# VectorE's order at the start of an attention and FFN kernel, and what TensorE multiplies only to be busy

## The chip, the cores and the metric

The kernel runs on one core of a Trainium2 chip. A core has engines with a queue of instructions each: TensorE (PE, matrix products; PEld is its loading of the stationary operand), VectorE (DVE), ScalarE (ACT), GpSimd (POOL) and SyncE (SP), which here issues nearly all transfers. Engines wait for each other through semaphores. The metric is the device time of one launch in microseconds; lower is better.

## The reference

For each of 8 batches and 8 heads, 576 positions of q, k and v (64 wide) go through a feature map with 128 random features, linear attention, and then a two-layer FFN over all 4,608 tokens.

```python
def phi(x):
    proj = np.einsum('bhsd,md->bhsm', x, omega)
    sq = np.sum(x * x, axis=-1, keepdims=True) / 2.0
    h = proj - sq
    h = h - np.max(h, axis=-1, keepdims=True)
    return np.exp(h) / np.sqrt(m)
q_p, k_p = (phi(q_s), phi(k_s))
kv = np.einsum('bhsm,bhsd->bhmd', k_p, v)
z = np.sum(k_p, axis=2)
num = np.einsum('bhsm,bhmd->bhsd', q_p, kv)
den = np.einsum('bhsm,bhm->bhs', q_p, z)[..., None] + 1e-06
x = num / den                       # as (4608, 512)
h = x @ w_in                        # 512 x 2048
g = h * np.tanh(softplus(h))
out = g @ w_out                     # 2048 x 512
```

## The kernel before

Tokens go in 36 query tiles of 128 (`q0` to `q35`) and 18 FFN blocks of 256. Keys go by batch and pair of heads (`k0_0` is batch 0, pair 0). Most products take operands that are split into two float16 parts; the first work runs on float32 instead, because the splits need scales that are not known yet: all keys of batches 0 and 1 and the queries of tiles 0 to 4, their products with the values, and FFN block 0.

**A key or query tile** (`features`, L376): the load is popped from those made at the start; TensorE multiplies it with `om_f` into banks of PSUM (`pk`, `pq`, L416); VectorE takes the maximum of each row (L426); ScalarE takes the exponentials with the maximum as bias (L431). In the float32 tiles two to five (`1 < nth < 6`: k0_2, k0_3, q0, q1), `spin(1, ident, e...)` (L443) then multiplies a part of the result by the identity into a bank that nobody reads. `spin` (L98) issues such unread products; there are also ten at the start, eight behind the second key tile (L422), both from the constant `idle`, and two behind the x of tile 1 (L709). The function ends with `anchors[nth] = (last.ins, sub.ins)`: the tile's last exponential (ScalarE) and its last maximum (VectorE).

**Keys** then go into a product with the values (`pkv`, L490), which ScalarE copies out (L496). **Queries** (`q_first`, L658): TensorE transposes the exponentials (`pt`, L665), ScalarE copies them (L666), TensorE multiplies them with the key-value sums (`pn`, L676), VectorE divides (L680 to L692) into `x`; for tiles 0 and 1, TensorE transposes x (`px`, L703) and ScalarE copies it to `xT` (L704). That is what the first FFN product (`ph`, L770) needs, together with w_in.

**w_in** comes in eight blocks of 1 MB, w0 to w7 (`w_task`, L200): ScalarE brings one part of each word into place (L211), VectorE shifts the other (L213), joins the two by an or (L217) and takes the block's maximum (L221). From all eight maxima comes the scale by which the blocks are split for the float16 blocks that follow. The values of batch 0 have a like step: `v_task` (L309) takes four maxima (L319) and from them a scale.

**Order.** The program is written as a list of generators that are stepped slot by slot (`step`, L1190); a yield says in how many slots a generator goes on. FIRST, WIS and WOS (L1135 to L1137) say in which slot a tile or weight block starts. Within a slot the generators go in the order in which they were put on the list: first `v_task(0)`, then the weight blocks, then the key and query tiles, which are put on it later. A planner then orders each engine's queue: among instructions that it counts as ready, the earlier in the program goes first; the engine executes that order as it stands. `with behind(nth, first)` (L194) adds an order without a semaphore: what is issued inside comes, on its own engine, behind the instructions `anchors[nth][first:]` of the same engine. The tables AV, AN, AM, AO, AP (L1141 to L1145) say for each block behind which anchor its steps come: AV for the values' maxima, AN for the shift and the or, AM for the blocks' maxima, AP for ScalarE's step. `anchors[30 + t]` is the x of tile t on VectorE, `anchors[100 + t]` its copy on ScalarE.

**Transfers.** PREL (L1149) lists the first loads: keys, values, q0, q1, then the eight blocks of w_in; q2, q3 and the values of batch 1 follow on the same queue.

**PSUM.** The pool `ps_a` has four banks and serves pk, pq, pkv, pt, pn and px; `ps_h` (two) serves ph and one bank of each of the first key tiles; `ps_o` (two) serves the FFN's outputs and the spins. The exponentials lie in two buffers (tag `ae`).

Of the kernel before, what the change touches and what calls it, by code (L numbers as in the profile page):

```python
# [30 lines left out]
def tile_kernel(  # L31
# [10 lines left out]
    nc = tc.nc  # L42
    P = 128
# [27 lines left out]
    def cast(eng, out, in_, scale=1.0):  # L71

        if eng is act:
            act.activation(out, in_, AF.Copy, scale=scale)  # L74
        elif isinstance(scale, float) and scale == 1.0:
            eng.tensor_copy(out, in_)  # L76
        else:
            eng.tensor_scalar_mul(out, in_, scale)
# [16 lines left out]
    idle = const.tile([P, 512], F16, name="idle")  # L95
    dve.memset(idle, 1.0)

    def spin(n, left, right):  # L98
        pi = ps_o.tile([P, 512], F32, tag="o", name=f"spin{nc.next_id()}")
        for _ in range(n):  # L100
            nc.tensor.matmul(out=pi[:, 0:right.shape[1]], lhsT=left, rhs=right, start=True, stop=True)
# [3 lines left out]
    ident = const.tile([P, P], F32, name="ident")  # L105
# [87 lines left out]
    @contextmanager  # L193
    def behind(nth, first=0):  # L194
        with ExitStack() as st:
            for ins in anchors.get(nth, ())[first:]:
                st.enter_context(tc.issue_after(ins))
            yield

    def w_task(i, name):  # L200

        n = 0 if name == "wi" else 1
        raw = loaded.pop(f"w{n}_{i}", None) or fetch_w(n, i, w_dma)
        yield W_LOAD
        word = raw.bitcast(I32).rearrange("p (n two) -> p n two", two=2)
        low, high = word[:, :, 0], word[:, :, 1]
        dst = flat32(slots[w_at(n, i)])
        di = dst.bitcast(I32)
        with behind(AP[i] if n == 0 else None):
            m = high.bitcast(F32)  # L210
            act.activation(m, m, AF.Prelu, scale=2.0 ** -112, alpha=-(2.0 ** 32))  # L211
        with behind((AN, AO)[n][i]):
            dve.tensor_single_scalar(out=di, in_=low, scalar=29, op=ALU.logical_shift_right)  # L213
        yield W_GAP
        did("w", n, i)
        with behind((AN, AO)[n][i]):
            dve.scalar_tensor_tensor(  # L217
                out=di, in0=high, scalar=3, in1=di, op0=ALU.logical_shift_left, op1=ALU.bitwise_or
            )
        with behind(AM[i] if n == 0 else None):  # L220
            dve.tensor_reduce(  # L221
                out=wmax[n][:, i:i + 1], in_=dst, axis=AX.X, op=ALU.max, apply_absolute_value=True
            )
# [70 lines left out]
    for i in range(2):  # L294
        t = const.tile([P, 2, 10, D1], F16, name=f"vb{i}")
# [13 lines left out]
    def v_task(b):  # L309
        vt = []  # L310
        for hp in range(HP):
            vt.append(loaded.pop(f"v{b}_{hp}", None) or fetch_v(b, hp))
        if b == 0:
            vstate[0] = (vt, None, None)
        yield 3 if b else 6
        mx = sb.tile([P, HP], F32, tag="vmx", name=f"vmx{b}", bufs=2)
        for hp in range(HP):
            with behind(AV if b == 0 else None, 1):
                dve.tensor_reduce(  # L319
                    out=mx[:, hp:hp + 1], in_=vt[hp][:, :, 0:D], axis=AX.XY, op=ALU.max,  # L320
                    apply_absolute_value=True,
                )
            yield 0 if hp % 2 == 0 or b == 0 else 1
        am = sb.tile([P, 1], F32, tag="vam", name=f"vam{b}")
        if b < 2:
            with tc.high_priority(PRIO):
                dve.tensor_reduce(out=am, in_=mx, axis=AX.X, op=ALU.max)
                p, s = pow2(am, f"v{b}", TOP)
        else:
            dve.tensor_reduce(out=am, in_=mx, axis=AX.X, op=ALU.max)  # L330
            yield 1
            p, s = yield from pow2_pe(am, f"v{b}", TOP)
        vstate[b] = (vt, p, s)
# [5 lines left out]
    anchors = {}  # L339
# [36 lines left out]
    def features(load, tiles, name, nth, whole):  # L376

        f = loaded.pop(name, None) or (  # L380
            fetch_pair if whole else fetch_tails if name[0] == "k" else fetch
        )(load, name)
        yield gap("load", name)
        if not whole:
            terms = yield from in_parts(f, name, nth)
        n = sum(len(g) for g in tiles)
        by_act = whole
        e = sb.tile([P, n, M], F32, tag="ae", name=f"e{name}", bufs=2)
        mx = sb.tile([P, n], F32, tag="mx", name=f"mx{name}")
        pps, lo = [], 0  # L390
        for g in tiles:
            own, tag = (ps_h, "h") if nth < HP and len(pps) == 2 else (ps_a, "a")
            pp = own.tile([P, 4, M], F32, tag=tag, name=f"p{name}_{lo}")
            pps.append((pp, lo, lo + len(g)))
            lo += len(g)
            if whole:
                continue
            for i, parts in enumerate(g):
                for rows, o in parts:
                    for j, (left, right) in enumerate(terms):  # L400
                        nc.tensor.matmul(  # L401
                            out=pp[rows, i, :], lhsT=left[:, o:o + rows.stop - rows.start],
                            rhs=right, start=j == 0, stop=j == len(terms) - 1,
                        )
        if whole:

            w = f.shape[1]
            order = [(g, i) for i in range(4) for g in (0, -1)] + [(1, 0)] * (len(tiles) - 2)
            mm = None
            for g, i in order:  # L410
                for rows, o in tiles[g][i]:
                    a = slice(o // w * D, (o // w + 1) * D)
                    with ExitStack() as st:
                        if mm is not None:
                            st.enter_context(tc.issue_after(mm.ins))
                        mm = nc.tensor.matmul(  # L416
                            out=pps[g][0][rows, i, :], lhsT=f[a, o % w:o % w + rows.stop - rows.start],
                            rhs=om_f[a], start=True, stop=True,
                        )
            if nth == 1:  # L420
                with tc.issue_after(mm.ins):
                    spin(8, idle[:, 0:P], idle)  # L422
        yield 1
        for pp, lo, hi in pps:
            m = hi - lo
            sub = dve.tensor_reduce(  # L426
                out=mx[:, lo:hi], in_=pp[:, :m, :], axis=AX.X, op=ALU.max, negate=by_act
            )
            if by_act:
                for i in range(m):  # L430
                    last = act.activation(  # L431
                        e[:, lo + i, :], pp[:, i, :], AF.Exp, bias=mx[:, lo + i:lo + i + 1]
                    )
            else:
                sub = dve.tensor_tensor(  # L435
                    out=e[:, lo:hi, :], in0=pp[:, :m, :],
                    in1=mx[:, lo:hi].unsqueeze(2).broadcast_to([P, m, M]), op=ALU.subtract,
                )
        yield gap("exp", name)
        if not by_act:  # L440
            last = act.activation(e, e, AF.Exp, bias=lnt)  # L441
        elif 1 < nth < 6:
            spin(1, ident, e[:, 0:2, :].rearrange("p n m -> p (n m)"))  # L443
        anchors[nth] = (last.ins, sub.ins)
        return e

# [95 lines left out]
    def q_task(nth, t):  # L542
# [5 lines left out]
        e = yield from features(qT[t], tiles, f"q{t}", nth, t < QF)  # L548
        if t < QF:
# [9 lines left out]
            out=qp.rearrange("p a h s -> p (a h) s"), in_=qn.rearrange("p a h m -> p (a h m)")  # L559
# [18 lines left out]
        for g, pn in enumerate(pns):  # L578
# [10 lines left out]
                out=x[:, hs, :], in0=pn[:, :, 0:D], in1=rd[:, hs].broadcast_to([P, 4, D]),  # L589
                op=ALU.mult,  # L590
            )
        anchors[30 + t] = (xt.ins,)
        yield from x_parts(nth, t, x)

    x_more = {}
# [62 lines left out]
    def q_first(nth, t, e, off):  # L658

        qp = sb.tile([P, H, P], F32, tag="ap", name=f"qp{t}", bufs=2)  # L660
        for g in range(2):
            hs = slice(4 * g, 4 * g + 4)
            pt = ps_a.tile([P, 4, P], F32, tag="a", name=f"pt{t}_{g}")
            for i in range(4):
                nc.tensor.transpose(out=pt[:, i, :], in_=e[:, 4 * g + i, :], identity=ident)  # L665
            cast(act, qp[:, hs, :], pt)  # L666
        yield 1
        x = sb.tile([P, H, D], F32, tag="x", name=f"x{t}", bufs=2)
        rd = sb.tile([P, H, 1], F32, tag="rd", name=f"rd{t}")
        for g in range(2):  # L670
# [20 lines left out]
            for b, lo, hi in spans(t * P, P):  # L691
# [1 line left out]
                    out=x[lo:hi, hs, :], in0=pn[lo:hi, :, 0:D], scalar=vstate[b][2][lo:hi],  # L693
                    in1=rd[lo:hi, hs].broadcast_to([hi - lo, 4, D]), op0=ALU.mult, op1=ALU.mult,
                )
        anchors[30 + t] = (xt.ins,)
        if t * P >= CH:
            yield from x_parts(nth, t, x)
            return
# [433 lines left out]
    w_dma = nc.sync  # L1133

    FIRST = (0, 1, 2, 3, 4, 4, 9, 9, 19, 21, 24, 27, 32, 36, 43, 58, 59, 68)  # L1135
    WIS = (3, 4, 5, 6, 7, 8, 9, 10)
    WOS = (28, 27, 26, 25, 24, 23, 22, 21)  # L1137
    WI0, FF0, V0, V1 = 0, 17, 0, 16
    W_LOAD, W_GAP, PRIO = 1, 1, 400

    AO = (None,) * 8  # L1141
    AV = 3
    AN = (None,) * 5 + (31,) * 3
    AM = (None,) * 3 + (31,) * 5
    AP = (None,) * 7 + (101,)  # L1145

    W_LO = ('dddddddd', 'dddddddd')
# [91 lines left out]
    for what in PREL.split():  # L1239
        i = int(what[1:] or 0)  # L1240
# [105 lines left out]
```

## Time and profile before

| what | value |
| --- | --- |
| median of three runs | 939.56 us (939.08 to 940.1) |
| the profiled execution | 939.57 us |
| its span, from the first to the last instruction | 937.8 us |
| mean granted clock of TensorE | 0.993 |

An execution on the chip is recorded instruction by instruction. The page of the profile gives the busy time of each engine, the chain of work that ended last, and groups of instructions. Lines of a timeline read: start, length, engine, line, operation, what is written and from what, shapes, count, and in brackets how long the engine had been idle before it and what ended that. Instructions of one engine can overlap by a fraction in the record, so a group's time is better read from one start to the next. Rows of windows give busy times in a stretch of the span, the TensorE clock that was granted (1.00 is full), the share of the transfer engines and GB/s.

### The profile page before, as it was taken

Reading aid. Unit: us, or ns where it says so; the run is one execution under the profiler, and the core shown is the slowest. Engines: PE = TensorE matmul, PEld = TensorE weight load, DVE = VectorE, ACT = ScalarE, POOL = GpSimd, SP = SyncE. Lnnn points to the kernel's source line nnn. Section 1 sums busy time; section 2 is a strip of 40 time slices with the busy share of each in tenths; the row PEclk is TensorE's granted clock in tenths of the full one; section 3 lists DMA queues with packets and bytes.
Section 4 is the critical chain, followed back from the end, with each engine's and each line's share of the span. In section 5 each row is a group of like instructions: output and inputs, shape, how many; then the busy total and the mean of one; then the engine's idle time right before and its main releaser. Section 6 shows DMA issues by size and latency. Waiting matters only on the chain. (4 is left out here: it accounts for less than half of the span.)

```text
span 937.8 us, 21111 instructions
## 1 busy us (share of the span) xinstructions
PE 920.5 (98%) x8795; PEld 689.4 (74%) x8795; DVE 707.1 (75%) x1234; ACT 658.9 (70%) x873; POOL 213.6 (23%) x134
## 2 busy tenths in 40 slices
PE   9799989999999999999999999999999999999998
PEld 6688765677777777777777777777777777679997
DVE  5799898685678688787688857878688756658774
ACT  6568966678777878778677776788786866345442
POOL 0000023242342224321333134231241232200000
PEclk9799999999999999999999999999999999999999
DMA  9766325443442256323543265523533156973521
GB/s 308 264 227 215 108 58 93 99 83 75 95 107 85 80 115 128 90 81 76 107 114 97 69 120 107 126 60 93 112 73 91 35 114 141 210 218 92 162 66 45
DMA packets 153055, 108.69 MB, mean 116 GB/s; under 512 B 112832, under 2 KB 125248, under 8 KB 152960
## 3 DMA queue, kind: packets, MB, share of 16 engines
q1 hardware_dynamic: 152640, 106.75, 44.6%
q8 instruction: 69, 1.13, 0.5%
q10 hardware_dynamic: 320, 0.59, 0.2%
q14 instruction: 26, 0.21, 0.1%
HBM read 63.14 MB, written 17.83 MB: 86 GB/s over the span
## 5 line engine op out<-in xcount | busy, mean ns | idle before, releaser
L770 PE MATMUL ph<-xT,w 128*128 128x256 f16 (+1 forms) x2816 | 342.2, 278 | 0.0
L1097 PE MATMUL po<-wo,g 128*128 128x512 f16 x1344 | 308.5, 379 | 0.0
L770 PEld LDWEIGHTS <-w 128*128 128x128 f16 x2688 | 260.7, 98 | 46.1 <-issue 0.6
L1097 PEld LDWEIGHTS <-g 128*128 128x128 f16 x1344 | 127.2, 98 | 132.7
L83 POOL TENSOR_TENSOR sq<-fq,sq 64x1024 f16<-64x1024 f32 x31 | 70.5, 2275 | 253.6 <-ACT sq L74 177.8
L955 ACT ACTIVATE h<-ph,us 128x512 f32<-128x512 f32 (+3 forms) x152 | 83.2, 573 | 49.7 <-PE ph L770 48.5
L85 DVE SCALAR_TENSOR_TENSOR g<-h,us,g 128x1024 f16<-128x1024 f32 (+3 forms) x76 | 99.9, 1325 | 15.2 <-ACT g L74 14.9
L83 POOL TENSOR_TENSOR sk<-fk,sk 64x1152 f16<-64x1152 f32 x24 | 59.3, 2469 | 91.6 <-ACT sk L74 79.3
L83 POOL TENSOR_TENSOR xs<-x,xs 128x512 f16<-128x512 f32 (+1 forms) x35 | 40.7, 1164 | 153.0 <-DVE xs L76 102.0
L955 ACT ACT_TABLE_LOAD x56 | 71.8, 1283 | 1.0
L441 ACT ACT_TABLE_LOAD x53 | 68.0, 1283 | 4.2 <-DVE ek L435 3.3
L426 DVE TENSOR_REDUCE mxq<-pq 128x4 f32<-128x512 f32 x72 | 46.7, 682 | 24.8 <-PE pq L401 23.9
L83 DVE TENSOR_TENSOR qn<-eq,qn 128x1024 f16<-128x1024 f32 x31 | 39.2, 1263 | 29.9 <-ACT qn L74 29.9
L906 PEld LDWEIGHTS <-w 128*128 128x128 f16 x1008 | 59.0, 98 | 3.3 <-issue 0.7
L441 ACT ACTIVATE ek<-ek,lnt 128x1152 f32<-128x1152 f32 x24 | 30.1, 1256 | 42.3 <-DVE ek L435 42.2
L74 ACT ACTIVATE g<-h,us 128x1024 f16<-128x1024 f32 (+3 forms) x64 | 58.2, 932 | 0.8
L426 DVE TENSOR_REDUCE mxk<-pk 128x4 f32<-128x512 f32 (+1 forms) x96 | 49.5, 546 | 7.3 <-PE pk L416 3.5
L83 DVE TENSOR_TENSOR kp<-ek,kp 128x1152 f16<-128x1152 f32 x24 | 32.8, 1366 | 27.0 <-ACT kp L74 26.2
L1044 PEld LDWEIGHTS <-gb 128*128 128x128 f16 x504 | 48.3, 98 | 5.2
L83 POOL TENSOR_TENSOR vb<-vf,vb 128x640 f16<-128x640 f32 x24 | 37.3, 1554 | 55.2 <-DVE vb L76 41.5
L955 ACT ACTIVATE h<-h,us 128x1024 f32<-128x1024 f32 (+2 forms) x16 | 14.7, 930 | 48.6 <-DVE h L915 48.6
L441 ACT ACTIVATE eq<-eq,lnt 128x1024 f32<-128x1024 f32 x31 | 35.6, 1149 | 18.8 <-DVE eq L435 18.5
(185 smaller groups left out, 1370.3 us busy)
## 6 DMA issues: line engine op xcount, KB each, us to landing
w<-ds SPq DMA_DIRECT2D x48, 256.0 KB, 3.6
vf<-in_vL_dram SPq DMA_DIRECT2D x32, 325.0 KB, 3.3
out_dram<-o SPq DMA_DIRECT2D x36, 256.0 KB, 2.3
fq<-in_qT_dram SPq DMA_DIRECT2D x31, 256.0 KB, 3.5
fk<-in_kT_dram SPq DMA_DIRECT2D x24, 256.0 KB, 3.6
raw<-in_w_out_dram SPq DMA_DIRECT2D x5, 1024.0 KB, 7.8
wo<-in_w_in_dram SPq DMA_DIRECT2D x4, 1024.0 KB, 10.6
raw<-in_w_in_dram SPq DMA_DIRECT2D x4, 1024.0 KB, 15.3
```

The lines of the kernel that those rows point to most:

```text
L74: act.activation(out, in_, AF.Copy, scale=scale)
L83: eng.tensor_tensor(out=out, in0=in_, in1=hi, op=ALU.subtract)
L85: eng.scalar_tensor_tensor(out=out, in0=in_, scalar=scale, in1=hi, op0=ALU.mult, op1=ALU.subtract)
L426: sub = dve.tensor_reduce(out=mx[:, lo:hi], in_=pp[:, :m, :], axis=AX.X, op=ALU.max, negate=by_act)
L441: last = act.activation(e, e, AF.Exp, bias=lnt)
L770: nc.tensor.matmul(out=ph[:, i, :], lhsT=wi(a, k, f) if c else wi0(k, f), rhs=xT[c][:, y, k, :] if c else xT0()[:, k, :], start=n == 0, st ...
L906: nc.tensor.matmul(out=ph[:, i, :], lhsT=left(gr, op_l, i, a, k), rhs=x_region(c, r)[:, y, k0 + k, :], start=n == 0, stop=n == len(mm) - 1,)
L955: act.activation(h[:, :, lo:hi], ph[:, :, lo:hi], AF.Mish, scale=us[:, 0:1])
L1044: nc.tensor.matmul(out=ps, lhsT=gT[c, n][:, i, a, f, :], rhs=rhs, start=f == 0 and (a, y) == (1, 0), stop=f == FG - 1 and (a, y) == (0, 0),)
L1097: nc.tensor.matmul(out=po[i], lhsT=gT[c, gr][:, a, f % FG, i * P:(i + 1) * P], rhs=wo(y, f), start=f == 0 and (a, y) == parts[0], stop=f = ...
```

## The change

Three things are rewritten at the start of the kernel.

VectorE's order: `AN` is split into `AS` (for the shift) and `AN` (for the or). w0's or and maximum and w1's shift now come behind the last maximum of tile 3 (k0_3); w1's or and maximum, w2's shift and maximum, and the values' maxima (AV) behind the last maximum of tile 5 (q1). Blocks 5 to 7 stay behind the x of tile 1 (31). All blocks of w_in start one or two slots later (WIS), the values' maxima one slot later.

`behind` for VectorE's steps now takes the anchor's second entry (`first=1`), so `anchors[30 + t]` gets a `None` in front.

The unread products: the four that read exponentials are removed; behind the transposes of query tiles 0 and 1 come four each from the constant `idle`, 512 wide.

```diff
-        with behind((AN, AO)[n][i]):
+        with behind((AS, AO)[n][i], 1):
             dve.tensor_single_scalar(out=di, in_=low, scalar=29, op=ALU.logical_shift_right)
         yield W_GAP
         did("w", n, i)
-        with behind((AN, AO)[n][i]):
+        with behind((AN, AO)[n][i], 1):
             dve.scalar_tensor_tensor(
...
-        with behind(AM[i] if n == 0 else None):
+        with behind(AM[i] if n == 0 else None, 1):
             dve.tensor_reduce(
...
-        yield 3 if b else 6
+        yield 3 if b else 7
...
-        elif 1 < nth < 6:
-            spin(1, ident, e[:, 0:2, :].rearrange("p n m -> p (n m)"))
         anchors[nth] = (last.ins, sub.ins)
...
-        anchors[30 + t] = (xt.ins,)
+        anchors[30 + t] = (None, xt.ins)
...
             for i in range(4):
-                nc.tensor.transpose(out=pt[:, i, :], in_=e[:, 4 * g + i, :], identity=ident)
+                tr = nc.tensor.transpose(out=pt[:, i, :], in_=e[:, 4 * g + i, :], identity=ident)
             cast(act, qp[:, hs, :], pt)
+        if t < 2:
+            with tc.issue_after(tr.ins):
+                spin(4, idle[:, 0:P], idle)
...
-    WIS = (3, 4, 5, 6, 7, 8, 9, 10)
+    WIS = (4, 6, 7, 8, 9, 10, 11, 12)
...
-    AV = 3
-    AN = (None,) * 5 + (31,) * 3
-    AM = (None,) * 3 + (31,) * 5
+    AV = 5
+    AS = (None, 3, 5) + (None,) * 2 + (31,) * 3
+    AN = (3, 5) + (None,) * 3 + (31,) * 3
+    AM = (3, 5, 5) + (31,) * 5
```

More of the change, by code (lines that the diff above doesn't have):

```diff
@@ L695, in q_first @@
                 )
-        anchors[30 + t] = (xt.ins,)
+        anchors[30 + t] = (None, xt.ins)
         if t * P >= CH:
```

## The prediction, made before the changed kernel was run

> **What bounds the kernel now.** The profiled execution took 939.57 us, 1.77 us more than its span, against a median of 939.56 us; a microsecond less of span is taken as one off the time. I read the page first, then TensorE's waits, windows around the longest wait, and the timelines of TensorE, VectorE and ScalarE there.
>
> ```profile
> span 937.8 us, 21111 instructions
> PE 920.5 (98%) x8795; PEld 689.4 (74%) x8795; DVE 707.1 (75%) x1234; ACT 658.9 (70%) x873; POOL 213.6 (23%) x134
> ...
> PE spin L101 <- ACT eq L431: 6.9, 1, 6.9
> ...
> 22.70:29.60 6.90, 0.00 (x1) 0.01 (x1) 6.63 (x14) 3.31 (x7) 0.62 (x1) 0.64 1.06 389
> 29.60:38.30 8.70, 8.70 (x36) 7.85 (x36) 6.96 (x8) 5.03 (x14) 0.00 (x0) 0.50 1.06 327
> 160.00:937.80 777.80, 772.56 (x7751) 577.02 (x7748) 571.15 (x995) 542.69 (x660) 197.41 (x109) 1.00 0.43 102
> ...
> 24.00:25.00 1.00, 0.00 (x0) 0.00 (x0) 1.00 (x3) 0.18 (x1) 0.00 (x0) 0.84 1.04 385
> 38.00:39.00 1.00, 1.00 (x6) 0.53 (x5) 0.00 (x0) 1.00 (x4) 0.00 (x0) 0.84 1.03 330
> ```
>
> (Window rows: stretch, length, busy time of PE, PEld, DVE, ACT, POOL, granted clock, DMA share, GB/s.) TensorE bounds the kernel: behind 160 us it is busy 772.56 of 777.80 us. So time is won only where it stands still early, and there is one such place: it waits 6.9 us for the exponentials of q0, and the granted clock falls. 0.84 in 24 to 25 is full speed until 24.7 and half after, 2.0 us behind the last matmul; 0.84 in 38 to 39 puts the return at 38.3, after 8.7 us of work at half speed, half of which (4.35 us) is loss. Stall and clock together cost 6.9 + 4.35 = 11.3 us.
>
> ```profile
> 15.73 0.65 PE L101 MATMUL spin<-ek,ident 128*128 128x256 f32 x2
> 16.31 1.53 PE L416 MATMUL pk<-om_f,fk 64*128 64x128 f32 x20
> 17.76 2.45 PE L490 MATMUL pkv<-vf,ek 128*128 128x65 f32 x20
> 20.05 0.65 PE L101 MATMUL spin<-ek,ident 128*128 128x256 f32 x2
> 20.63 2.06 PE L416 MATMUL pq<-om_f,fq 64*128 64x128 f32 x32
> 29.60 1.22 PE L101 MATMUL spin<-eq,ident 128*128 128x256 f32 x2 [6.92 <-ACT eq L431]
> 30.61 4.37 PE L490 MATMUL pkv<-vf,ek 128*128 128x65 f32 x20
> 34.77 1.06 PE L665 MATMUL pt<-ident,eq 128*128 128x128 f32 x4
> 35.69 1.22 PE L101 MATMUL spin<-eq,ident 128*128 128x256 f32 x2
> 36.71 2.85 PE L665 MATMUL pt<-ident,eq 128*128 128x128 f32 x12
> ...
> 17.55 0.69 DVE L426 TENSOR_REDUCE mxk<-pk 128x4 f32<-128x512 f32 x1 [0.38 <-PE pk L416]
> 18.16 1.21 DVE L217 SCALAR_TENSOR_TENSOR w<-wo,w 128x1024 int32<-128x1024 int32 x1
> 19.29 0.28 DVE L426 TENSOR_REDUCE mxk<-pk 128x1 f32<-128x128 f32 x1
> 19.50 1.21 DVE L221 TENSOR_REDUCE wmax<-w 128x1 f32<-128x1024 f32 x1
> 20.62 0.68 DVE L213 TENSOR_SCALAR w<-wo 128x1024 int32<-128x1024 int32 x1
> 21.22 0.68 DVE L426 TENSOR_REDUCE mxk<-pk 128x4 f32<-128x512 f32 x1
> 21.82 2.98 DVE L319 TENSOR_REDUCE vmx<-vf 128x1 f32<-128x640 f32 x4
> 24.72 1.21 DVE L217 SCALAR_TENSOR_TENSOR w<-wo,w 128x1024 int32<-128x1024 int32 x1
> 28.14 0.68 DVE L426 TENSOR_REDUCE mxq<-pq 128x4 f32<-128x512 f32 x1
> ...
> 28.92 2.17 ACT L431 ACTIVATE eq<-pq,mxq 128x128 f32<-128x128 f32 x8 [1.99 <-DVE s_v L127]
> 35.02 0.62 ACT L431 ACTIVATE eq<-pq,mxq 128x128 f32<-128x128 f32 x2 [2.88 <-PE pkv L490]
> ```
>
> The products of q0 and q1 are there at 22.69, but VectorE takes their first maximum at 28.14. Ahead of it stand the values' maxima (2.98 us) and shift, or and maximum of w_in's blocks. That is an order of the queue, not lack of data, and the change rewrites it.
>
> **The old spins go.** Four spins hang on exponentials. The first two take 0.58 us each from start to next start (15.73 to 16.31, 20.05 to 20.63); the two on eq take 1.0 us each at half clock, 0.5 at full. Without the first two, pk of k0_3 starts at 15.7 and the products of q0, q1 end at 22.69 - 1.16 = 21.5. Pool `ps_a` has four banks; counted through the code, the values' product of k0_3 needs a bank that q0's first four exponentials free. So removing the spin alone doesn't remove the wait (gain of that alone between 0 and 1.2 us).
>
> **The new order on VectorE.** w0's or and maximum and w1's shift now come behind k0_3's maxima, which then end near 15.7 + 1.2 (16.31 to 17.55) + 0.69 + 0.28 + 0.68 = 18.5 instead of 21.9. w0's pair, earlier in program order than q0's maxima, probably still goes first: 18.5 + 1.2 + 1.2 = 20.9. q0's first maximum is then at 20.9; its bounds are 20.5 (half of the products done, nothing ahead) and 21.5 (w1's shift too). The first four exponentials take half of 2.17: 21.6 to 22.7. The values' product of k0_3 runs from 22.7, 7.9 us earlier than 30.61, at full clock in 2.3 us (17.76 to 20.05), to 25.0. TensorE's stall shrinks from 6.9 to 1.2 us, below the 2.0 us after which the clock fell, so I take the clock as full.
>
> **The rest of the way to FFN block 0.** eq of q1 waits for that product (2.88 us in its row) and still will.
>
> ```profile
> 39.39 3.68 PE L676 MATMUL pn<-kvf,qp 128*128 128x65 f32 x32
> 45.18 0.48 PE L416 MATMUL pq<-om_f,fq 64*128 64x128 f32 x2
> 45.60 0.70 PE L770 MATMUL ph<-xT,w 128*128 128x256 f32 x2
> 46.23 2.05 PE L416 MATMUL pq<-om_f,fq 64*128 64x128 f32 x30
> ...
> 7.98 1.90 PE L101 MATMUL spin<-idle 128*128 128x512 f16 x8
> 9.96 0.17 DVE L146 MEMSET idle<- 1x128 f32 x1 [0.77 <-PE spin L101]
> ```
>
> From the end of the product (34.77) to the first ph (45.60) are 10.83 us. Half clock until 38.3 makes up 3.53 / 2 = 1.77 us of it; an old spin of 0.5 goes; eight new ones come, 1.90 us by the row of eight. They read only a constant and stand where TensorE waits for ScalarE to copy pt and finish q1's exponentials, so their cost lies between 0 and 1.9; I take 1.4. The memset of `idle` at 9.96 must now wait for them, 0.2 us of VectorE beside the x chain. The first ph: 25.0 + 10.83 - 1.77 - 0.5 + 1.4 = 35.0, which is **10.6 us earlier**.
>
> **What is moved behind.** The four values' maxima and w1's or and maximum, w2's shift, wait behind q1's last maximum, about 23.4 (20.9 + four of 0.6 from start to start); behind them on VectorE stand w2 to w4 and then q0's x. The value loads of batch 1 wait for those tiles, but SP reaches them only at 29.51. w1 is read by ph's third f, well behind 35. If its order is bad, one such instruction (1.2 us) stands ahead of x; between 0 and 1.2, taken as 0 because x is earlier in program order.
>
> **How much of 10.6 us reaches the end.** TensorE is the bound later, but VectorE is nearly as full in between.
>
> ```profile
> 17.50:44.10 26.60, 19.45 (x137) 17.19 (x138) 21.36 (x41) 16.64 (x39) 0.62 (x1) 0.74 0.93 319
> 44.10:160.00 115.90, 112.44 (x777) 83.80 (x775) 108.02 (x184) 89.56 (x145) 14.32 (x10) 1.00 0.47 139
> ```
>
> VectorE's work up to 44.1 fills 21.36 of 26.60 us: it can come only 5.2 us earlier. From there to 160 it idles 7.88 us more, which it may give up. So its shift lies between 5.2 and 13.1, TensorE's is 10.6. I let VectorE give up half: 5.2 + 3.9 = 9.1 us. Fillers for TensorE (FFN block 0's products, the other products of block 1) are at hand meanwhile, so VectorE's lag isn't all paid: 5.2 is the low end, 10.6 the high. **Forecast: 939.6 - 9.1 = 930.5 us, 929 to 934.4.**
>
> **Rivals.** *A load becomes the wait.* In TensorE's order the first products of q2 stand ahead of the first ph (45.18 before 45.60).
>
> ```profile
> L361 SPq DMA_DIRECT2D fq<-in_qT_dram x4: 589/596/2585, 25.0 to 28.9; - x4
> 29.51 8.95 SPq L306 DMA_DIRECT2D vf<-in_vL_dram  x4
> DMA to landing us min/median/max: 11.4/11.6/13.8
> ```
>
> These loads of q2 and q3 are issued behind all of w_in (first at 25.0, last at 28.9) and land at 25.0 + 13.8 = 38.8, the last at 28.9 + 11.4 = 40.3. Before, that was early enough; now TensorE could stand at q2 from 35.0 to 38.8, 3.8 us, over the 2.0 after which the clock fell. Against it: the queue orders are planned, and a planner that counts this load late puts ph first. The first ph would be near 40.3, a gain of 5.3 where the clock holds; at half for 8.7 us of work, as here, it costs 4.35 of them, gain 0.95. Between the two, **936.4 us**. [...] *Slower:* the same stall, but the clock stays at half as long as here, 24.7 to 38.3 = 13.6 us: 6.8 lost, 5.3 - 6.8 = -1.5, **941.1 us**. The load decides once the stall at q2 exceeds 2.0 us, and the sign turns once the clock stays at half for more than 2 x 5.3 = 10.6 us.
>
> [...]
>
> *The change doesn't bite*: the planner takes what is ready, w blocks slip ahead of q0 as before, and only the spins count: gain 0 to 1.2, **939.0 us**.
>
> **How the numbers follow.** Forecast 0.60; more than 10.6 us (idle later also filled, down to 926.5) 0.05; load without the long half clock 0.14; clock falls 0.08; doesn't bite 0.04; slower 0.09. 0.2% is 1.9 us, about what a measurement tells from no change. Faster: 0.60 + 0.05 + 0.08 and 0.09 of the load's 0.14, 0.82; same: its other 0.05 and the 0.04, 0.09; slower: 0.09. The range 926.5 to 937.0 takes in the forecast, its better tail, the fallen clock and half of the load; the rest is 0.20.
>
> **What would show it.** Right: mxq of q0 near 21, directly behind w0's or k0_3's work; no TensorE gap over 2 us from 15 to 45; granted clock 1.00 in every microsecond from 10 on; first ph near 35; the same landmarks at 160 us some 9 us earlier. Wrong: a wait of pq for fq near 35 to 39; a clock below 1 in 25 to 50; VectorE's last maximum of w_in less than 5 us earlier; or new waits of TensorE between 60 and 160 that add up to more than 5 us.

## The result, and the profile after

| | before | after |
| --- | --- | --- |
| median | 939.83 us (939.08 to 940.65, 6 runs) | 946.08 us (943.88 to 948.07, 6 runs) |
| the profiled execution | 939.57 us | 947.22 us |
| its span | 937.8 us | 945.4 us |
| its mean granted clock | 0.993 | 0.990 |

The ratio is 1.0064 [1.0053, 1.0074]: the change makes the kernel about 6 us slower. The six runs of after spread over 4.2 us, and the fastest (943.88) is the one with the highest mean clock (0.993); the others have 0.988 to 0.990. A kernel's queues are planned once, the falls of its clock differ from execution to execution (mean clock 0.988 to 0.993 in these six). At a mean clock of 0.993, the commonest in before (939.8 and 940.0 us, the medians of 13 such runs in each of the two sets below), after's one run still takes 4 us more, so the clock is only a part of the difference.

First TensorE's waits in the profile of after (who waited for whom: us in total, times, longest):

```profile
PE pn L570 <- DMA qp<-qn: 5.3, 3, 4.3
PE pn L570 <- DVE ek L435: 2.9, 1, 2.9
PE pk L416 <- ACT ek L431: 2.5, 1, 2.5
PE pkv L488 <- ACT eq L431: 1.6, 1, 1.6
```

The wait of 6.9 us at the start is gone but for 1.6. Three longer ones stand in its place, all of them later: for exponentials of a key tile, for a transposed operand, and for a key tile from which VectorE takes the maxima off (`ek`, L435). TensorE's timeline of after shows where:

```profile
1.47 4.45 PE L101 MATMUL spin<-idle 128*128 128x512 f16 x10 [1.47 <-DVE idle L96]
20.45 2.06 PE L416 MATMUL pq<-om_f,fq 64*128 64x128 f32 x32
24.11 2.56 PE L488 MATMUL pkv<-vf,ek 128*128 128x65 f32 x20 [1.61 <-ACT eq L431]
40.61 3.72 PE L771 MATMUL ph<-xT,w 128*128 128x256 f32 x16 [0.25 <-ACT xT L705]
...
76.06 1.52 PE L416 MATMUL pk<-om_f,fk 64*128 64x128 f32 x18 [2.51 <-ACT ek L431]
77.51 4.53 PE L488 MATMUL pkv<-vf,ek 128*128 128x65 f32 x20
91.58 8.96 PE L771 MATMUL ph<-xT,w 128*128 128x256 f32 x64
...
142.82 1.50 PE L570 MATMUL pn<-kv,qp 128*128 128x65 f16 x24 [4.26 <-DMA qp<-qn]
160.95 0.92 PE L570 MATMUL pn<-kv,qp 128*128 128x65 f16 x24 [0.52 <-DMA qp<-qn]
389.76 0.55 PE L570 MATMUL pn<-kv,qp 128*128 128x65 f16 x12 [2.85 <-DVE ek L435]
```

and the same landmarks of before:

```profile
1.47 3.66 PE L101 MATMUL spin<-idle 128*128 128x512 f16 x10 [1.47 <-DVE idle L96]
77.37 1.52 PE L416 MATMUL pk<-om_f,fk 64*128 64x128 f32 x18
78.82 2.45 PE L490 MATMUL pkv<-vf,ek 128*128 128x65 f32 x20
89.71 8.96 PE L770 MATMUL ph<-xT,w 128*128 128x256 f32 x64
139.88 0.92 PE L572 MATMUL pn<-kv,qp 128*128 128x65 f16 x24 [1.87 <-DMA qp<-qn]
156.42 0.92 PE L572 MATMUL pn<-kv,qp 128*128 128x65 f16 x24 [0.30 <-DMA qp<-qn]
```

The first row of each is the same work in both kernels, ahead of all that was changed; it took 0.8 us longer in this execution of after (4.45 against 3.66). Such a scatter shows in the experiments below as well: e3, e7 and e8 differ from after only in steps that come later, and their products of q0 start at 19.97, 21.02 and 20.90 (20.45 in after). So after's profile starts 0.8 us late by chance.

The lead can be followed from landmark to landmark. At the first `ph` after is 45.60 - 40.61 = 5.0 us ahead. At the run of 64 `ph` it is 1.9 us behind (91.58 against 89.71): 6.9 us went in 50. At the second of the two float16 `pn` it is 4.5 us behind (160.95 against 156.42). At 389 us come 2.85 us of waiting that before doesn't have (its counterpart there is 0.3 us), and the end is 7.6 us behind.

The same place shows twice what a wait costs beside its length: `pkv` takes 4.53 us in after and 2.45 in before. In the windows of after (columns as in the prediction) the clock is seen to fall behind the first two of the waits:

```profile
26.00:27.00 1.00, 1.00 (x8) 1.00 (x8) 1.00 (x3) 0.13 (x1) 0.00 (x0) 0.65 1.07 393
33.00:34.00 1.00, 1.00 (x8) 0.71 (x6) 0.00 (x0) 1.00 (x3) 0.00 (x0) 0.94 1.05 387
77.00:78.00 1.00, 1.00 (x9) 0.71 (x8) 1.00 (x2) 1.00 (x3) 0.00 (x0) 0.75 0.37 142
84.00:85.00 1.00, 1.00 (x5) 0.37 (x3) 1.00 (x3) 1.00 (x6) 0.00 (x0) 0.84 0.32 122
...
160.00:945.40 785.40, 777.45 (x7785) 579.58 (x7783) 575.62 (x1004) 544.26 (x662) 199.35 (x110) 1.00 0.42 102
```

0.65 in 26 to 27 puts the fall at 26.3, 0.94 in 33 to 34 the return at 33.1: 6.83 us at half. 0.75 in 77 to 78 and 0.84 in 84 to 85 give 77.5 to 84.3, again 6.83 us. A third stretch of 3.41 us begins at 142.35, at the wait for tile 5's operand. The wait of 2.85 us at 389 is followed by none: the clock is 1.00 from 386 to 392. The granted clock in these stretches is 0.50, so where TensorE is busy throughout I count half of the length as lost: 3.4 us at the second. In the 50 us between 40.6 and 91.6, the wait of 2.51 and 3.4 of clock make 5.9 of the 6.9 us that went; at the third stretch the wait of 4.26 (1.87 in before) comes on top of 1.7.

Behind 160 us after stands still for 785.40 - 777.45 = 7.95 us, before for 5.24: 2.7 us more, as much as the one wait at 389. Most of the rest of the 7.6 is the 4.5 that it was already behind.

VectorE's and ScalarE's timelines say why TensorE had to wait with its lead. In before:

```profile
54.98 1.21 DVE L221 TENSOR_REDUCE wmax<-w 128x1 f32<-128x1024 f32 x1
76.12 2.43 ACT L431 ACTIVATE ek<-pk,mxk 128x128 f32<-128x128 f32 x9
133.23 1.05 ACT L74 ACTIVATE qn<-eq 128x1024 f16<-128x1024 f32 x1
```

and in after:

```profile
17.86 1.49 DVE L426 TENSOR_REDUCE mxk<-pk 128x4 f32<-128x512 f32 x3 [0.34 <-PE pk L416]
21.00 1.22 DVE L221 TENSOR_REDUCE wmax<-w 128x1 f32<-128x1024 f32 x1
22.13 2.48 DVE L426 TENSOR_REDUCE mxq<-pq 128x4 f32<-128x512 f32 x4
34.73 0.16 DVE L681 TENSOR_SCALAR rd<-pn 128x4 f32<-128x4 f32 x1 [3.81 <-PE pn L677]
37.91 1.19 DVE L221 TENSOR_REDUCE wmax<-w 128x1 f32<-128x1024 f32 x1
55.07 1.19 DVE L221 TENSOR_REDUCE wmax<-w 128x1 f32<-128x1024 f32 x1
126.34 0.69 DVE L435 TENSOR_TENSOR eq<-pq,mxq 128x512 f32<-128x512 f32 x1
127.55 3.06 DVE L85 SCALAR_TENSOR_TENSOR wo<-wo,s_w 128x1024 f16<-128x1024 f32 x1
130.54 0.68 DVE L435 TENSOR_TENSOR eq<-pq,mxq 128x512 f32<-128x512 f32 x1
...
74.86 2.44 ACT L431 ACTIVATE ek<-pk,mxk 128x128 f32<-128x128 f32 x9
130.65 1.15 ACT L74 ACTIVATE wo<-wo,s_w 128x1024 f16<-128x1024 f32 x1 [2.89 <-DVE wo L85]
136.16 1.05 ACT L74 ACTIVATE qn<-eq 128x1024 f16<-128x1024 f32 x1
```

VectorE takes q0's first maximum 6.0 us earlier (22.13, was 28.14), but w_in's last maximum at 55.07 instead of 54.98, not earlier at all. The exponentials of k1_0 come 1.3 us earlier (74.86 against 76.12). TensorE would be at that place 3.8 us earlier (76.06 - 2.51 = 73.55, against 77.37), and 2.5 of the 3.8 are the wait. ScalarE had no room to be earlier there: its timeline shows no idle time from 64.03 to 74.86.

The loss at tile 5 is of another kind. There TensorE waits although it has no lead any more: the split of its operand (`qn`) is made 2.9 us later than before, since ScalarE stood behind a weight block that it waited for VectorE to finish. VectorE's queue has that block (127.55) between the two halves of tile 5's `eq`; before has both halves first and the block behind them.

### The profile page after: what moved, and what is told of

It is laid out like the page before. It is cut to its first block, busy times and chain, and to the rows that moved or that the text cites. A ratio compares the mean times of both kernels' runs of the same rounds, so it can differ in the third digit from the quotient of the medians.

```text
span 945.4 us, 21108 instructions
## 1 busy us (share of the span) xinstructions
PE 924.6 (98%) x8795; PEld 691.0 (73%) x8795; DVE 706.4 (75%) x1234; ACT 656.0 (69%) x871; POOL 216.1 (23%) x134
## 5 line engine op out<-in xcount | busy, mean ns | idle before, releaser
L83 POOL TENSOR_TENSOR vb<-vf,vb 128x640 f16<-128x640 f32 x24 | 38.5, 1605 | 56.4 <-DVE vb L76 44.2
## 6 DMA issues: line engine op xcount, KB each, us to landing
wo<-in_w_in_dram SPq DMA_DIRECT2D x4, 1024.0 KB, 10.6
```

Source lines behind the costliest of these rows:

```text
L83: eng.tensor_tensor(out=out, in0=in_, in1=hi, op=ALU.subtract)
```

## The experiments

Two questions stood: does the order or the spins cost the time, and is it the wait at k1_0 with its clock that eats the lead? The theory: TensorE's lead is worth nothing, because VectorE and ScalarE are not ahead; it runs into their results at 74 us and later, and such a wait can take the clock down for some microseconds more (6.83 us at half behind the 2.51 at k1_0 in after). The rivals: the spins displace work; or the order does harm by itself; or the transposed operand of tile 5 is the cause. The first four kernels were measured beside before at 940.46 us (29 runs), the last four beside 939.83 (23 runs).

### The order alone, the spins alone

`e1_order_only` has the new order, with the old four spins and without the new ones; `e2_spins_only` has the order of before and the new spins in place of the old.

```diff
 (e1, against after)
+        elif 1 < nth < 6:
+            spin(1, ident, e[:, 0:2, :].rearrange("p n m -> p (n m)"))
...
-        if t < 2:
-            with tc.issue_after(tr.ins):
-                spin(4, idle[:, 0:P], idle)
```

> The new order on VectorE with the four old unread products on exponentials kept and the eight new constant ones left out. Theory (clock and waits): the changed kernel gains 5.0 us up to the first ph and gives it back where TensorE now arrives before ScalarE and VectorE (2.5 us wait at 73.5 us, clock at half behind it; 4.3 us wait at 138.6 us), so the order alone should show the same: first ph near 40 to 42 us, slower than before by 2 to 8 us. Rival (the new unread products do the harm): the order alone is no slower than before, 0 to 5 us faster. Rival (re-planning): the early part as in the theory, but the end anywhere between -5 and +8 us, with long waits at other places.

> The old order on VectorE with the new constant products in place of the old ones. Theory: the 6.9 us wait for q0's exponentials stays (5.5 to 7 us, before the values' product of k0_3), the clock falls as before, first ph at 44.5 to 46.5 us, the time within 2 us of before. Rival (the new unread products do the harm): slower than before by 4 us or more. Rival (re-planning): first ph as in the theory, the end up to 5 us off in either direction.

Measured: the order alone 940.92 us, ratio 1.0007 [0.9998, 1.0016]; the spins alone 939.35 us, 0.9998 [0.9983, 1.0012]. Neither part alone changes the time measurably. For the order alone the theory had expected 2 to 8 us more than before, so that is a miss; the time is the one that its first rival gave. TensorE's timeline of the order alone:

```profile
72.01 2.33 PE L416 MATMUL pk<-om_f,fk 64*128 64x128 f32 x18 [1.89 <-ACT ek L431]
140.24 1.18 PE L572 MATMUL pn<-kv,qp 128*128 128x65 f16 x24 [4.92 <-DMA qp<-qn]
```

and of the spins alone:

```profile
30.82 4.53 PE L488 MATMUL pkv<-vf,ek 128*128 128x65 f32 x20 [7.92 <-ACT eq L431]
91.66 8.96 PE L771 MATMUL ph<-xT,w 128*128 128x256 f32 x64
```

With the order alone the clock holds at the start (granted 1.00 from 10 to 70 us; the wait there is 1.2 us) and the first `ph` comes at 37.76, 7.8 us ahead. Then the wait for k1_0's exponentials is 1.89 us, the clock is at half from 72.4 to 82.7 (10.24 us, 5.1 lost), and tile 5's operand is waited for 4.92 us: the lead is gone at 140 us (140.24, before 139.88). So even a lead of 7.8 us is given back whole. The spins alone leave the start as it was, with 7.92 us of waiting; that excludes that unread products do harm by themselves. With the new order the exchange of the spins is not free, since it is the only edit between e1 and after, which is 5 us slower. Without the old spins the wait at the start is 1.61 instead of 1.19 us, the clock falls, and the first `ph` comes 2.9 us later (0.8 of it by the late beginning); the wait of 2.85 us at 389, which e1 doesn't have, is about the rest.

The spins alone show one thing more. They begin the run of 64 `ph` at 91.66, as late as after (91.58), and yet are no slower than before: at tile 5 they wait 1.35 us for the operand and the clock stays (1.00 from 45 to 170 us). So what happens up to 91 us takes the lead away, but doesn't by itself make a kernel slower than before.

### Holding the clock at one place or the other

Unread products from a constant, which touch no output, were added at two places. `e3_hold_start` puts eight behind q1's products, where the 1.61 us of waiting were. `e4_hold_k1` puts twelve behind the `ph` of FFN block 0 with f = 11, just ahead of k1_0's wait. `e5_hold_start_k1` does both.

```diff
-            if nth == 1:
+            if nth in (1, 5):                       (e3, e5)
                 with tc.issue_after(mm.ins):
                     spin(8, idle[:, 0:P], idle)
...
+                    if c == 0 and f == 11:          (e4, e5)
+                        with tc.issue_after(mm1.ins):
+                            spin(12, idle[:, 0:P], idle)
```

> The changed kernel and eight more constant products behind the products of q1, in the 1.6 us gap after which its clock fell at 26.65 us. Theory: the clock stays full from 10 to 40 us, the first ph comes 2.5 to 3.5 us earlier than in the changed kernel (near 37 to 38), VectorE's idle time of 3.8 us ahead of the first rd shrinks below 1 us and its last maximum of w_in comes 2 to 3.5 us earlier than 55.07 us; of the time 2 to 4 us are gained against the changed kernel (942 to 944 us). Rival (VectorE and ScalarE bind in any case): first ph earlier, but exponentials of k1_0 still at 74 to 75 us and no gain at the end. Rival (re-planning): the early part as in the theory, the end unrelated, +-5 us.

> The changed kernel and twelve more constant products (2.6 us) behind the product of FFN block 0 that comes last before the 2.5 us wait at 73.5 us. Theory: that wait shrinks below 0.6 us, the clock stays full from 70 to 90 us where it was at half for 6.4 us, and the values' product of k1_0 takes 2.4 instead of 4.5 us: 2.5 to 3.5 us gained against the changed kernel at 92 us, and 942 to 944 us in all if nothing else moves. Rival (the half clock there costs nothing because VectorE binds): clock full, but the next landmarks (first float16 ph of block 1 at 91.6 us, first po at 100.4 us) unchanged within 0.7 us. Rival (re-planning): landmarks to 100 us as in the theory, the end unrelated.

> The changed kernel with both sets of constant products: eight behind q1's products and twelve behind the FFN block 0 product that comes last before the wait for k1_0's exponentials. Theory (waits at k1_0 and q5, with the clock): first ph near 38 us, clock full up to 130 us, no TensorE wait over 1 us from 50 to 130, first po of block 0 (100.37 us in the changed kernel, 98.51 before) at 95.5 to 97.5 us; the q5 wait may stay. 936 to 940 us in all. Rival (VectorE and ScalarE bind everything behind 50 us): first po no earlier than 98.5. Rival (re-planning): early landmarks as in the theory, the end unrelated, 936 to 946 us.

Measured:

| kernel | us | ratio to before | first `ph` | at half clock (start us, length) |
| --- | --- | --- | --- | --- |
| before | 940.46, 939.83 | | 45.60 | 24.67, 13.65 |
| after | 946.08 | 1.0064 [1.0053, 1.0074] | 40.61 | 26.3, 6.83; 77.5, 6.83; 142.35, 3.41 |
| e3_hold_start | 942.91 | 1.0031 [1.0019, 1.0043] | 37.98 | 73.1, 10.24; 141.36, 3.41 |
| e4_hold_k1 | 940.08 | 0.9998 [0.9985, 1.0012] | 43.45 | 25.8, 10.24; 831.35, 3.41 |
| e5_hold_start_k1 | 939.25 | 0.9989 [0.9976, 1.0002] | 38.49 | 152.57, 3.41 |

The last two columns are of the profiled execution alone; that of e4 is the slowest of its twelve (943.62 us), those of e3 and e8 are the fastest of theirs (942.00 and 941.82). The times of e3 and e5 are as expected, that of e4 is lower than expected.

Each hold does what it is for, and alone there: e3 has no fall at the start (granted clock 1.00 from 10 to 70 us), e4 none at k1_0 (1.00 from 40 to 100). From the first `ph` to the first `po` after takes 59.8 us and e3 61.1; e4 takes 56.4 (43.45 to 99.87) and e5 56.6, with 2.6 us of useless products in them. With those taken off the way is 6 us shorter than in after, as much as the wait at k1_0 and its clock come to there (2.5 + 3.4). e4 as a whole is 6.0 us faster than after, and its runs show what the clock costs where the order of the queues is one and the same: they go from 936.88 us at a mean clock of 0.998 to 943.62 at 0.992.

But the hold changed something else too. In e4 VectorE has both halves of tile 5's `eq` in one piece again:

```profile
125.26 1.28 DVE L435 TENSOR_TENSOR eq<-pq,mxq 128x512 f32<-128x512 f32 x2
```

So do before, e2, e5, e6 and e8, where tile 5's operand is waited for 1.9 us or less; after, e1, e3 and e7 have the weight block in between, with a wait of 3.4 to 4.9 us and a fall of the clock there. These four are also the ones that lose the clock at k1_0, so no run has one without the other, and how much of the 6.0 us belongs to which place is not shown.

In TensorE's timeline of e3 the wait at k1_0 is the same as in after although the start is mended:

```profile
73.44 2.69 PE L416 MATMUL pk<-om_f,fk 64*128 64x128 f32 x18 [2.53 <-ACT ek L431]
```

With both, TensorE waits nowhere over 0.5 us from 50 to 130 us. A window and rows of its timeline:

```profile
44.10:100.00 55.90, 55.75 (x376) 44.00 (x373) 51.55 (x86) 43.78 (x80) 0.70 (x2) 1.00 0.62 204
95.08 2.84 PE L1118 MATMUL po<-wo,g 128*128 128x512 f32 x6
132.17 0.92 PE L570 MATMUL pn<-kv,qp 128*128 128x65 f16 x24 [1.34 <-DMA qp<-qn]
152.40 1.40 PE L570 MATMUL pn<-kv,qp 128*128 128x65 f16 x24 [2.18 <-DMA qp<-qn]
```

The first `po` comes at 95.08, where before has it at 98.51 and after at 100.37. At tile 5's `pn` the lead over before is 7.7 us (132.17 against 139.88), at tile 6's 4.0 (152.40 against 156.42): here too it is given back, at a wait of 2.18 us and a fall of the clock, only later. (The queues differ in what stands ahead of these steps. By an estimate from the products done until then and their mean times, before has 2.5 us more work behind it at tile 5's `pn`, so e5's lead in work is about 5 us there.) Two more waits (1.49 us for a transposed operand at 789, 1.73 for VectorE at 828) take part of the rest. The median of 939.25 us has an interval that includes no change: the holds undo the loss, but they win nothing that can be told.

### The holds with the old spins

`e6_order_k1` is the order alone with the twelve products at f = 11.

> The new order with the old unread products on exponentials, and the twelve constant products ahead of k1_0's wait. Theory: first ph near 37.8 us as with the order alone, the 1.9 us wait at 70 us and the half clock from 72.6 to 82 us gone, first po at 94 to 96.5 us instead of 97.8; 936 to 939 us in all, faster than the order alone (940.9) by 2 to 5 us. Rival (re-planning): first po as in the theory, the end anywhere from 936 to 945.

Measured: 940.18 us, ratio 1.0004 [0.9995, 1.0014]; the first `po` at 98.07. That is a miss. The wait was not gone, it went one step on, to an FFN product that needs a bank freed by ScalarE:

```profile
79.09 0.70 PE L770 MATMUL ph<-xT,w 128*128 128x256 f32 x2 [2.41 <-ACT g L74]
```

The clock fell behind it too (80.9, for 3.41 us). In e6 TensorE only waits for ScalarE one step later; e4 and e5, with the same hold, show no such wait.

### Tile 5's operand

`e7_q5_later` has TensorE come to tile 5's `pn` some slots later, with other work ahead of it.

```diff
-        yield 2
+        yield 5 if t == 5 else 2
```

> The changed kernel with the products of q5 three slots later, so that three more FFN products stand ahead of its 4.3 us wait for the transposing transfer at 138.6 us. Theory: all as in the changed kernel up to 138 us (first po at 100.4), the wait of 4.3 us below 1.5 us and no half clock at 142 to 146: 3 to 5 us gained against the changed kernel, 941 to 943 us. Rival (that wait is only where TensorE's lead shows and costs nothing): the wait goes and the time stays above 944.5.

Measured: 945.38 us, ratio 1.0061 [1.005, 1.0073]; 0.7 us under after, where 3 to 5 were expected: a miss. That `pn` no longer waits, but another of TensorE's steps does, some microseconds ahead of it, and the clock falls for 3.41 us as it does in after (last row):

```profile
24.67 2.45 PE L488 MATMUL pkv<-vf,ek 128*128 128x65 f32 x20 [1.60 <-ACT eq L431]
...
38.83 3.72 PE L771 MATMUL ph<-xT,w 128*128 128x256 f32 x16 [0.25 <-ACT xT L705]
...
74.28 1.78 PE L416 MATMUL pk<-om_f,fk 64*128 64x128 f32 x18 [2.51 <-ACT ek L431]
75.98 4.53 PE L488 MATMUL pkv<-vf,ek 128*128 128x65 f32 x20
...
135.81 0.38 PE L148 MATMUL every_v<-one_v,idle 1*128 1x1 f32 x2 [3.36 <-DVE one_v L139]
```

So it isn't the transposed operand alone: in both kernels the step of TensorE that meets VectorE's results first waits (4.26 us in after, 3.36 in e7). But the loss at this place stayed (3.36 us and the clock), and VectorE's queue still has the weight block between the halves of `eq`. That VectorE's order here makes after slower than before is therefore a rival that e7 doesn't test.

The other rows are of use too, since up to there TensorE's queue is that of after. The gap at the start is 1.60 us, the clock did not fall behind it (1.00 from 10 to 75 us), and from `pkv` to the first `ph` are 14.16 us; in after, with the fall, 16.50 (24.11 to 40.61). The fall at the start is thus worth 2.3 us, not the 3.4 of its half length: part of it lies in waits for ScalarE. And at k1_0 the wait is 2.51 us as in after, with 10.24 us at half clock (from 75.35): most of what is won at the start is lost there.

### Later on purpose

If the lead itself is what does harm, then after should become faster when TensorE is held up. `e8_late_on_purpose` adds 20 unread products ahead of the first `ph`, 4.3 us of work that serves nothing.

```diff
         if t == 1:
             for hs in (slice(0, 4), slice(4, 8)):
                 spin(1, ident, x[:, hs, :].rearrange("p h d -> p (h d)"))
+            spin(20, idle[:, 0:P], idle)
```

> The changed kernel with twenty useless constant products (4.3 us) ahead of the first ph. Theory (TensorE arrives too early at k1_0's exponentials and pays more than its lead): first ph near 45 us, the 2.5 us wait at 73.5 us falls below 1 us, the clock stays full from 70 to 90, first po at 98.5 to 101 us, so no later than in the changed kernel; the whole is no slower than the changed kernel, 941 to 946 us. Rival (TensorE's work binds from the first ph on): 4.3 us slower, 949 to 951 us, first po at 104 to 105.

Measured: 942.75 us, ratio 1.0039 [1.0024, 1.0054], 3.3 us faster than after. Its timeline:

```profile
74.86 1.52 PE L416 MATMUL pk<-om_f,fk 64*128 64x128 f32 x18
87.19 8.96 PE L772 MATMUL ph<-xT,w 128*128 128x256 f32 x64
154.61 1.50 PE L570 MATMUL pn<-kv,qp 128*128 128x65 f16 x24 [3.02 <-DMA qp<-qn]
```

The row at 74.86 has no wait in brackets: TensorE comes there with the exponentials made (ScalarE's first group at 73.60). The clock did not fall at the start, as in e7_q5_later, so these two can be compared without that chance: e8 is 2.6 us faster by the medians (942.75 against 945.38; the six runs of each overlap) with 4.3 us more work. At k1_0 e7 waits for 2.51 us and loses the clock for 10.24, e8 does neither (clock 1.00 from 10 to 150 us): its run of 64 `ph` begins 4.1 us ahead of e7's (91.33). Against after it is 4.4 us (87.19 against 91.58). At tile 6's operand e8 then waits 3.02 us, with 6.83 us at half clock. The order of VectorE's queue at tile 5 is not that of e7 either, so the gain at the end can't be put down to k1_0 alone.

## Why the prediction was wrong

The forecast was 930.5 us, the range 926.5 to 937.0, and 0.09 stood on slower; 946.08 lies 9 us above the range. What failed is the step from a lead at the first `ph` to a gain at the end, of which at least 5.2 us were to arrive. In one sum, by the profiles: of the forecast lead of 10.6 us, 5.6 are missing at the first `ph`, 6.9 are lost by the run of 64 `ph` (k1_0), 2.6 by tile 6's `pn` (tile 5's operand), and 3.1 behind it (the wait at 389 above all): 18.2 in all, so 7.6 us slower. By the same estimate from the products done, 0.9 of the 3.1 belongs to tile 5. Step by step, as the prediction has them:

- **The old spins go** (0 to 1.2 us): right. The products of q0 start only 0.2 us earlier (20.45, before 20.63), but after's profile began 0.8 us late; from the first products of k0_2 to those of q0 are 7.67 us (12.78 to 20.45) instead of 8.64, 1.0 less.
- **The new order on VectorE**: right in kind. q0's first maximum comes directly behind w0's maximum, but at 22.13, not 20.9 or at most 21.5; k0_3's maxima end 0.9 us later than counted (19.35), nearly all of it the late beginning, and a shift (w1's) goes first as well, which the upper bound allowed for. The rest of the stall is 1.6 us, not 1.2.
- **"Below the 2.0 us after which the clock fell, so I take the clock as full"**: failed. 2.0 us was one reading of one gap and no threshold: a gap of 1.61 us took the clock down in after, one of 1.71 in e4, and gaps of 1.60 in e7 and e8 did not. It cost 2.3 us. The chance of 0.08 on "clock falls", also in the range as "the fallen clock", had the event and counted it as a gain. No run shows the term behind it; what the runs showed is a fall of 6.83 us behind the gap of 1.61 us in after, and a loss at the end.
- **The first `ph` 10.6 us earlier**: 5.0, and 5.6 are missing. `pkv` starts at 24.11 instead of 22.7 (1.4); the fallen clock takes 2.3; and the way from the end of that product to the first `ph`, forecast at 9.96 us, is 11.9 where the clock holds (26.95, the start of the transposes in e7, to 38.83), 1.9 more. Of the 1.4, 0.8 is the late beginning. Of the 1.9, the new spins are not the cause: the way takes 11.0 us in e1, which doesn't have them, at full clock, no less than the 10.83 of before at half clock up to 38.3. So the 1.77 us that were taken off for the clock did not come. TensorE waits in it for ScalarE's copies (0.7 us) and for the last x (0.6 us), and ahead of that x VectorE takes the maximum of a w block (37.91, 1.19 us). That is the term that the prediction put at 0, "because x is earlier in program order".
- **"VectorE's shift lies between 5.2 and 13.1"**: the step that took the gain away. The end of VectorE's w_in work came 0.1 us later in after. The 5.2 was idle time in 17.5 to 44.1, counted as if the work could close up; but 3.78 us of it is the idle ahead of `rd`, which waits for TensorE's `pn`, and that stayed (3.81). Where the clock holds at the start, it shrinks (1.46 in e7 and e8, 0.52 in e3), and in e3 w_in's last maximum comes at 52.44, 2.5 us earlier, while TensorE is 7.6 ahead. So even then less than half of the 5.2 came.
- **"VectorE's lag isn't all paid"**, with 5.2 as the low end: failed. TensorE's lead was spent where its queue has a step that waits for ScalarE or VectorE (2.51 us at k1_0 in after, 1.89 in e1, 2.53 in e3); other products existed, but stood behind it in the order that was planned. The price of a wait was counted as at most the lead. With the fall of the clock it was more (2.51 us at k1_0, and 3.4 on top as half of the 6.83): after had 5.0 us and was 1.9 behind at the run of 64 `ph`. And that the order of VectorE's and ScalarE's queues 90 us later would change with the edit, and put tile 5's operand 2.9 us later, was no term of the sum.
- **The load of q2** as the new wait, with the rival on the slower side: it did not occur. The planner put sixteen `ph` ahead (40.61 to 44.26). The slower side came in a like way (a wait with a fall of the clock behind it, 2.51 and 6.83 us at k1_0; "the sign turns once the clock stays at half" long enough), at another place, 35 us later; the 0.09 had the direction, but not the cause.

Of the signs named, "VectorE's last maximum of w_in less than 5 us earlier" and "a clock below 1 in 25 to 50" came. The new waits between 60 and 160, "more than 5 us", came to 4.9 in the rows shown (2.51, and 4.26 less the 1.87 of before): with a new one of 0.52 at 126 (for ScalarE's `h`) to 5.4. So that sign came too, barely, and it left out the clock, which doubled them (3.4 + 1.7).

Shown by the runs: that the wait at k1_0 and its clock take the lead (the rows of after, and the shorter way from the first `ph` to the first `po` in e4 and e5), what the fall at the start costs (e7 against after), that the spins do no harm with the old order (e2), and that leads of 7 to 8 us at the first `ph` are given back by the end (e1, e3, e5, e6). Not shown is why after ends 6 us behind before rather than level with it. By its rows it is tile 5's operand with its clock and the wait at 389; e2, as late as after at 91 us, waits 1.35 and 0.6 us at these two places and is no slower than before. Both hang on the planned order of the queues, which came out differently with every edit at the start, and no run changed that order alone. The same holds for the waits at 789, 828 and 831 in e5 and e4.

## What to carry to other kernels

Before a stall on the bounding engine is valued at its length, find the next step in that engine's queue that waits for another engine, and ask whether that engine comes earlier too; idle time of the second engine that waits for the first doesn't count as room (3.78 us ahead of `rd` before, 3.81 after). Three short stalls cost more here (1.61, 2.51 and 4.26 us, with 17.07 us at half clock) than the long one that they replace (6.92 us, with 13.65). Look at the order of the other engines' queues far behind the edit as well: a planner may have changed it. And a version that holds the clock with useless work where a wait can't be removed (e4, e5: granted clock 1.00 from 45 to 100 us) is a cheap test of this, even if it wins nothing.

## What the runs showed of the hardware

Every stretch at half clock that ends within the span, in all nine kernels and in before (17 of them), is 3.41, 6.83, 10.24 or 13.65 us long, one to four times 3.41 us: 13.65 in before and e2; 10.24 in e1, e3, e4 and e7; 6.83 in e8 and twice in after; 3.41 in after, e1, e3, e4, e5, e7 and twice in e6. At the start the gap ahead of `pkv` had a fall behind it in after (1.61 us) and e4 (1.71) and none in e7 and e8 (1.60 each), and the longer one of 2.85 us at 389 in after had none either. So the length of a gap alone doesn't decide; what does is not shown.

The fall came with a delay at two places: in after the first gap ends at 24.11 and the clock falls at 26.3, in the second at 76.06 and 77.5, 2.2 and 1.4 us later, while TensorE is already at work again. The wait and the time at half clock add up there, they don't lie beside each other. At 142.35 it fell inside the gap, which ends at 142.82.
